# Order of the first four tiles, place of the third tile's v, and of the pad copies, in a fused attention and FFN kernel

## The chip, the cores and the metric

The kernel runs on one core of a Trainium2 chip. The metric is the device time of one execution in microseconds, as the median of several runs; lower is better. Engine names are those of the profile: PE is TensorE (PEld its weight loads), DVE is VectorE, ACT is ScalarE, POOL is GpSimd, SP is SyncE, which here only issues DMAs. A line number such as L169 is a line of the kernel before the change.

## What is computed

A transformer block of one sequence of S = 2048 rows of D = 448 in bfloat16: layer norm without parameters, then attention and a gated FFN in parallel, and the residual. There are 16 heads of 28; a query sees itself and the 255 keys before it. F is 1792.

```python
xn = (x - mean(x)) / sqrt(var(x) + 1e-5)
q, k, v = split(xn @ wqkv)                        # 16 heads of 28
scores = q @ k.T * 28 ** -0.5
scores = where((i - j >= 0) & (i - j < 256), scores, -1e9)
o = softmax(scores) @ v
out = x + o @ wo + (gelu(xn @ w_gate) * (xn @ w_up)) @ w_down
```

## The kernel before

The sequence is cut into 16 tiles of 128 rows and four blocks of 512 rows (`qb`). For each block the program runs attention (L561) and then the gated part of the FFN (`gated`, L452); the products with `wo` and `w_down` of a block run inside the attention of the next. The order of the instructions is written out by hand: each engine takes its own in the order of the program and stops at the first that has to wait. Each score step of attention makes scores (`sc`) in one PSUM tile of 4 banks, of which there is one during attention, and ScalarE turns them into `p_sb` with one exp of 128x2048. The entries of `plan` (L783) say what else is issued in a step, after its exp and its masks: a pair of a generator and a number takes that many pieces of the generator, a function is called.

*One tile's way.* `stat(t)` (L152) is a `bn_stats` and a `bn_aggr` on VectorE. `rstd(t, n)` (L157) is a Ln and an Exp on ScalarE, which give the inverse deviation of n tiles. `norm(t)` (L164) is a `tensor_scalar` on VectorE; for tiles over 3 there is a second one of 64 columns, on GpSimd for tiles 5, 6 and 7. Tiles 0 to 3 are then transposed by five PE instructions and copied out of PSUM by `transp` (L177), alternately through the banks "b2" and "b3", on ScalarE for tiles 0 to 2 and on VectorE for tile 3. Later tiles are transposed by a DMA on the SP queue, `dma_transp` (L173). `v_dense(t)` (L219) makes a tile's v from the first 384 of 448 input columns with three matmuls into a bank, `v_half` (L222) adds the last 64, and `v_copy` (L225) writes the result to `v_sb` and gives the bank back. `proj`, `qk_halves` and `qk_copies` do the same for q and k of a group of four heads; `pads` (L681) copies a group's weight columns into a layout of 32 columns a head.

*The start of the program (L692 to L740).* Ten matmuls on zeros (`warmup`), then tiles 0 to 3. In the order of the program the deviation of tile 2 comes after the transpose and copy of tile 0, that of tile 3 after the copy of tile 1. The pads of group 0 and the lower part of `w3p` stand between the normalizations and the last copy. GpSimd makes the masks after a small memset on VectorE (L716). `swap(0)` and the load of x tiles 8 to 11 are issued when tile 3 is transposed. The third tile's `v_dense` follows, then q and k of group 0, the statistics of tiles 4 and 5 and their deviations.

*The first block's steps.* Step 0 takes q and k of group 1 from `gen_qk` (L272), with both v halves of tiles 2 and 3 ahead of the q/k halves and the copy of tile 3's v after them; `ahead` normalizes and transposes tile 4. Step 1 takes group 2; `ahead2` has the statistics of tiles 6 and 7, tile 5's normalization and transpose, and the copy of tile 2's v. Step 2 takes group 3 and the first pieces of `gen_up`; its own exp stands behind `rstd(6, 2)` (L638); `ahead3` normalizes and transposes tiles 6 and 7 and then calls `loads` (L759), which issues on the SP queue, in this order: the rest of `w_up`, x tiles 12 to 15, `w_gate` in two parts (two DMAs each, one for each half of the partitions), `wo` and `w_down`. The masks of a step in the first block are `affine_select`s on GpSimd (L558), issued behind the step's exp and ahead of its plan. Step 3 ends `gen_up`; v of tiles 4 and 5, 6 and 7 comes from `gen_v` (L229). When attention of the block is over, `gated` starts with `up(0)` and `gate(0)`, whose matmuls `gt` read `wg`.

*Counters of DMAs.* The program's DMAs share eight completion counters in turn; a queue holds a DMA back until the earlier one of the same counter is complete.

Of the kernel before, what the change touches and what calls it, by code (L numbers as in the profile page):

```python
# [13 lines left out]
f32 = mybir.dt.float32  # L14
i32 = mybir.dt.int32

S, D, H, Dh, F = 2048, 448, 16, 28, 1792
P = 128
NT = S // P
NF = F // P  # L20
QB, NB = 512, 4
# [5 lines left out]
def kernel(  # L27
# [118 lines left out]
    def warmup(n):  # L146
        wps = phase[0].pool.tile([P, 2, QB], f32, name="wps", tag="s")
        for i in range(n):
            nc.tensor.matmul(wps[:, i % 2, :], lhsT=warm[:, 0:P], rhs=warm[:, 0:QB], start=True, stop=True)  # L149
# [7 lines left out]
    def rstd(t, n):  # L157
        lnv = work.tile([P, 4], f32, name="lnv")
        nc.scalar.activation(out=lnv[:, 0:n], in_=mv_all[:, t:t + n, 1], func=ACT.Ln, bias=eps_t[:, 0:1], scale=1.0)
        nc.scalar.activation(out=rstd_all[:, t:t + n], in_=lnv[:, 0:n], func=ACT.Exp, scale=-0.5)  # L160
# [61 lines left out]
    def v_half(t, pv):  # L222
        mm_half(pv, xnT[:, 3, t * P:(t + 1) * P], wv[:, 3, :], t % 2, False, True)

    def v_copy(t, pv, copy):  # L225
        copy(out=v_sb[:, t, :, 0:Dh], in_=pv.rearrange("p (h d) -> p h d", d=Dh))
        give(pv)
# [44 lines left out]
    def gen_qk(gs, others):  # L272

        for g in gs:
            pq = take("pq")
            proj(pq, wqp, 0, g)
            yield 650
            pk = take("pk")
            proj(pk, wkp, 0, g)
            yield 650  # L280
            for t, pv in others:
                v_half(t, pv)
            qk_halves(0, g, pq, pk)
            if others:
                v_copy(*others[1], nc.vector.tensor_copy)
            qk_copies(0, g, pq, pk)
            others = ()
            yield 360

    def fill_pads(last):  # L290
# [270 lines left out]
    def attention(qb, plan):  # L561
# [54 lines left out]
        for i, (scores, ncol, edges) in enumerate(steps):  # L616
            assert (qb, scores[-1][0]) in done
            if i in pvs:
                pv(pvs[i])
            while fresh:  # L620
                apply_masks(*fresh.pop(0))
            if not qb and i - 1 in pvs:
                sums()
                inverse()
            if qb == 3 and i - 1 in pvs:
                sums()
            ss = phase[0].pool.tile([P, 4, QB], f32, name="sc", tag="s")
            p_sb = work.tile([P, 4, QB], bf16, name="p_sb", bufs=5)
            for g, half, kt, q0, nq, col in scores:
                k0, nk = (64 * half, 64) if half is not None else (0, P)  # L630
                for j in range(4):
                    r = slice(32 * j, 32 * j + Dh)
                    nc.tensor.matmul(ss[k0:k0 + nk, j, col:col + nq], lhsT=kT[r, g, kt * P + k0:kt * P + k0 + nk],  # L633
                                     rhs=qT[r, g, ring(qb).start + q0:ring(qb).start + q0 + nq], start=True, stop=True,
                                     tile_position=(32 * j, k0), skip_group_check=True)
                parts.setdefault(g, []).append((half, kt, q0, nq, col, p_sb))
            if not qb and i == 2:
                rstd(6, 2)  # L638
            nc.scalar.activation(out=p_sb[:, :, 0:ncol], in_=ss[:, :, 0:ncol], func=ACT.Exp, scale=SCALE)  # L639
            flush()  # L640
            if qb:
                fresh.append((p_sb, edges))
            else:
                for m in edges:
                    masked(p_sb, *m)
            while later:
                scale_o(*later.pop(0))
            for n in plan[i]:
                if n == "sums":
                    sums()  # L650
                elif n == "inverse":
                    inverse()
                if not isinstance(n, tuple):
                    if callable(n):
                        n()
                    continue
                for _ in range(n[1]):
                    next(n[0], None)
            if qb == 3 and i - 2 in pvs:
                inverse()  # L660
# [28 lines left out]
        for _ in gen:  # L689
            pass  # L690

    warmup(10)  # L692
    stat(0)
    rstd(0, 1)
    stat(1)
    rstd(1, 1)
    norm(0)
    transp(0, nc.scalar.copy, "b2")
    stat(2)
    norm(1)  # L700
    rstd(2, 1)
    warmup(1)
    transp(1, nc.scalar.copy, "b3")
    stat(3)
    rstd(3, 1)
    pvs = [take("pv", D)]
    v_dense(0, pvs[0])
    norm(2)
    pads(nc.vector.tensor_copy, wqp, slice(0, 1))
    transp(2, nc.scalar.copy, "b2")  # L710
    pvs.append(take("pv", D))
    v_dense(1, pvs[1])
    norm(3)
    pads(nc.scalar.copy, wkp, slice(0, 1))
    nc.vector.tensor_copy(out=w3p[:, :, 0:Dh], in_=wraw[:, 3, 0:D].rearrange("p (h d) -> p h d", d=Dh))
    nc.vector.memset(masks[:, 0, 0, 0:1], 1.0)  # L716
    make_masks()
    transp(3, nc.vector.tensor_copy, "b3")
    swap(0)
    nc.sync.dma_start(out=x_sb[:, 8:12, :], in_=xv[:, 8:12, :])  # L720
    pvs.append(take("pv", D, "b2"))
    v_dense(2, pvs[2])
    pq, pk = (phase[0].pool.tile([P, 2, QB], f32, name="s0", tag="s")[:, 0, :] for _ in range(2))
    proj(pq, wqp, 0, 0)
    proj(pk, wkp, 0, 0)
    stat(4)
    stat(5)
    rstd(4, 2)
    qk_halves(0, 0, pq, pk)
    for t in range(2):  # L730
        v_half(t, pvs[t])
# [12 lines left out]
        dma_transp(4)  # L744

    def ahead2():
        stat(6)
        stat(7)
        norm(5)
        dma_transp(5)  # L750
        v_copy(2, pvs[2], nc.vector.tensor_copy)

    def ahead3():
        for t in (6, 7):
            norm(t)
            dma_transp(t)
        loads()
# [15 lines left out]
    for qb in range(NB):  # L773
        if qb in (1, 3):
            tc.mark_branch_hint_location("general", hint="LikelyTaken",
                                         engines=[mybir.EngineType.DVE if qb == 1 else mybir.EngineType.PE])
        early = ()
        if qb == 0:
            new_hT(0)
            early = (1, 2, 3)  # L780
            u = chain(gen_qk((1, 2, 3), [(t, pvs[t]) for t in (2, 3)]), gen_up(0, (1, 2)), gen_v(4, False), gen_up(0, (3,)),
                      gen_v(6, True), gen_qk_next())
            plan = [[(u, 2), ahead, (u, 1)], [(u, 2), ahead2, (u, 1)], [lambda: spare.append(spare.pop(1)), (u, 2), ahead3, (u, 4)],  # L783
                    [(u, 11), lambda: fill_pads(False)], [lambda: stat(8), (u, 10), lambda: fill_pads(True)], [(u, 3)],
                    [lambda: stat(9), (u, 4)], [lambda: stat(10), (u, 3)], [lambda: stat(11), (u, 3), lambda: rstd(8, 4)]]
        else:
            d = gen_down(qb - 1)
            if qb < 3:
                u = gen_pairs(qb + 1)
                plan = [[(d, 14)], [(d, 11)], [(d, 11)], [(u, 7)], [(d, 18)], ["sums", (u, 7), "inverse"], [(u, 12)],  # L790
                        [(u, 9)], [lambda: q_last(qb + 1, nc.vector.tensor_copy), (d, 5), "sums", "inverse"], [(d, 13)]]
                if qb == 1:
                    plan[0].append(lambda: rstd(12, 4))
            else:
                new_hT(3)
                early = (1, 2, 3, 4, 5, 6)
                u = gen_up(3, early)
                plan = [[(d, 14)], [(d, 4), (u, 5)], [(u, 9)], [(u, 7)], [(d, 18)], [(u, 7)], [(d, 13)], [(d, 5), (u, 7)],
                        [(u, 7)], [(d, 18)]]
        if qb in (1, 2):  # L800
            swap(qb + 1)
        if qb == 1:
            swap_weights(wvs, wv, wv)
            swap_weights(wsq, wqp, wkp)
            swap(1)
        score_pool(1)
        rest, after, flush = attention(qb, plan)
        nc.scalar.preload_act_table(ACT.Gelu_apprx_tanh)
        score_pool(2)
        if qb not in hTs:  # L810
            new_hT(qb)

        def hook(f):
            after(f)
            if qb < 3 and f == 4:
                collect(qb + 1)
            if qb < 3 and f == 10:
                deliver(qb + 1)
            t = 4 * qb + 8 + f // 2 - 2 * qb
            if qb < 2 and 4 * qb + 8 <= t < 4 * qb + 12:  # L820
                norm(t)
                dma_transp(t)
                if qb == 0:
                    stat(t + 4)

        gated(qb, early, rest, flush, hook)
        if qb < NB - 1:
            nc.scalar.preload_act_table_set("natural_log_exp_and_others")
# [151 lines left out]
```

## Time and profile before

| | us |
|---|---|
| median of 3 runs | 217.25 |
| lowest, highest of them | 216.87, 217.26 |
| the profiled execution | 217.55 |
| span of its instructions | 215.8 |
| PE busy (share of the span) | 210.3 (97%) |
| DVE busy | 156.8 (73%) |
| ACT busy | 131.6 (61%) |
| POOL busy | 48.1 (22%) |
| granted TensorE clock, mean | 0.999 |

The span runs from the first to the last instruction of one profiled execution; times in the lists below count from its start. A row of the timeline holds start, duration, engine, line, operation, what is written and read, and a count where like rows are merged; in brackets stand the idle time of the engine before it and what ended it. SPq is the queue that issues DMAs: its row is the issue, not the transfer. A row of the table by stretches holds, for PE, PEld, DVE, ACT and POOL, the busy time with the number of instructions, then the granted clock, the share of time in which the 16 DMA engines were busy, and GB/s.

### The profile page before, as it was taken

Reading aid. Unit: us, or ns where it says so; the run is one execution under the profiler, and the core shown is the slowest. Engines: PE = TensorE matmul, PEld = TensorE weight load, DVE = VectorE, ACT = ScalarE, POOL = GpSimd, SP = SyncE. Lnnn points to the kernel's source line nnn. Section 1 sums busy time; section 2 is a strip of 40 time slices with the busy share of each in tenths; the row PEclk is TensorE's granted clock in tenths of the full one; section 3 lists DMA queues with packets and bytes.
Section 4 is the critical chain, followed back from the end, with each engine's and each line's share of the span. In section 5 each row is a group of like instructions: output and inputs, shape, how many; then the busy total and the mean of one; then the engine's idle time right before and its main releaser. Section 6 shows DMA issues by size and latency. Waiting matters only on the chain.

```text
span 215.8 us, 6282 instructions
## 1 busy us (share of the span) xinstructions
PE 210.3 (97%) x2688; PEld 102.4 (47%) x2693; DVE 156.8 (73%) x348; ACT 131.6 (61%) x125; POOL 48.1 (22%) x81
## 2 busy tenths in 40 slices
PE   7999999999999999999999999999999999999993
PEld 2433433444445445444445545544444444444892
DVE  7788879799446997598547799567359699587621
ACT  4589589645876976613777797423578676466000
POOL 5278978520000202022000112022000021115001
PEclk9999999999999999999999999999999999999999
DMA  6993499993392000003330000200000000000011
GB/s 185 268 233 47 86 223 230 230 251 70 59 251 70 24 3 28 17 3 50 70 97 24 24 0 3 61 6 3 0 13 11 26 3 24 21 3 0 21 35 42
DMA packets 23553, 15.21 MB, mean 70 GB/s; under 512 B 9856, under 2 KB 23264, under 8 KB 23520
## 3 DMA queue, kind: packets, MB, share of 16 engines
q1 hardware_dynamic: 22576, 14.47, 29.1%
q8 instruction: 22, 0.36, 0.7%
q10 hardware_dynamic: 944, 0.29, 0.5%
q14 instruction: 11, 0.09, 0.1%
HBM read 8.69 MB, written 2.18 MB: 50 GB/s over the span
## 4 chain that ended last, share of the span: by engine, by line
PE 96%; ACT 2%; issue 1%; DVE 0%; DVEq 0%; ACTq 0%
PE po L392 26%; PE gt L432 20%; PE u L432 14%; PE ue L432 7%; PE sc L633 6%; PE ov L600 5%; PE pq L366 4%; PE pv L352 3%; PE pv L190 2%; PE wps L149 2%; PE pq L190 2%; ACT p_sb L639 2%; PE pk L190 1%; PE s L190 1%; PE pq L196 1%
## 5 line engine op out<-in xcount | busy, mean ns | idle before, releaser
L639 ACT ACTIVATE p_sb<-sc 128x2048 bf16<-128x2048 f32 x39 | 73.3, 1878 | 20.3 <-PE sc L633 14.8
L567 POOL TENSOR_TENSOR oN<-oc,l 128x512 bf16<-128x512 f32 x16 | 22.2, 1386 | 140.3 <-DVE l L580 140.3
L471 ACT ACTIVATE ge<-gt 128x1024 bf16<-128x1024 f32 x28 | 28.6, 1023 | 39.1 <-PE gt L432 33.9
L392 PE MATMUL po<-wd,hT 128*128 128x448 bf16 (+1 forms) x266 | 47.9, 324 | 0.0
L432 PE MATMUL gt<-xnT,wg 64*128 64x512 bf16 x224 | 45.4, 376 | 0.0
L432 PE MATMUL gt<-xsw,wg 64*128 64x512 bf16 x168 | 40.6, 376 | 0.0
L479 DVE TENSOR_TENSOR hT<-ge,u 128x512 bf16<-128x512 bf16 x38 | 24.5, 680 | 17.9 <-PE u L432 10.1
L548 DVE TENSOR_TENSOR p_sb<-p_sb,masks 128x256 bf16<-128x256 bf16 (+1 forms) x90 | 30.2, 389 | 5.9 <-ACT p_sb L639 5.9
L392 PEld LDWEIGHTS <-hT 128*128 128x128 bf16 x266 | 24.6, 98 | 16.0 <-issue 1.0
L432 PE MATMUL u<-xnT,wu 64*128 64x512 bf16 x152 | 31.7, 376 | 0.0
L432 PEld LDWEIGHTS <-wg 64*128 64x128 bf16 x392 | 19.6, 94 | 21.9 <-issue 0.2
L432 PEld LDWEIGHTS <-wu 64*128 64x128 bf16 x392 | 19.1, 94 | 23.0 <-issue 3.3
L432 PE MATMUL u<-xsw,wu 64*128 64x512 bf16 x114 | 27.2, 376 | 0.0
L400 DVE TENSOR_TENSOR res<-po,x_sb 128x448 bf16<-128x448 f32 (+1 forms) x17 | 10.1, 593 | 18.8 <-PE po L392 18.8
L633 PE MATMUL sc<-qT,kT 28*64 28x320 bf16 (+7 forms) x648 | 16.4, 261 | 0.3 <-ACT p_sb L639 0.2
L558 POOL TENSOR_SCALAR_AFFINE_SELECT p_sb<-p_sb 128x512 bf16<-128x512 bf16 (+1 forms) x21 | 14.2, 702 | 4.5 <-ACT p_sb L639 4.4
L432 PE MATMUL ue<-xnT,wu 64*128 64x512 bf16 x72 | 15.1, 377 | 0.0
L392 PE MATMUL po<-wo,oN 128*128 128x448 bf16 (+1 forms) x76 | 15.1, 323 | 0.0
L633 PEld LDWEIGHTS <-kT 28*64 28x64 bf16 (+1 forms) x648 | 7.7, 102 | 12.4 <-issue 10.8
L432 PE MATMUL ue<-xsw,wu 64*128 64x512 bf16 x54 | 13.5, 378 | 0.0
L448 DVE CAST hT<-ue 128x512 bf16<-128x512 f32 x18 | 11.5, 682 | 2.4 <-PE ue L432 2.4
L573 DVE STREAM_TRANSPOSE l<-oc 128x512 f32<-128x512 f32 x16 | 11.3, 705 | 1.6 <-POOL oN L567 1.6
(103 smaller groups left out, 253.3 us busy)
## 6 DMA issues: line engine op xcount, KB each, us to landing
out_dram<-res SPq DMA_DIRECT2D x15, 112.0 KB
xsw<-xnT SPq DMA_DIRECT2D x8, 192.0 KB
x_sb<-in_A_x_dram SPq DMA_DIRECT2D x3, 448.0 KB
wu<-in_B_w_up_dram SPq DMA_DIRECT2D x4, 336.0 KB
wd<-in_B_w_down_dram SPq DMA_DIRECT2D x3, 448.0 KB
wg<-in_B_w_gate_dram SPq DMA_DIRECT2D x2, 448.0 KB
wg<-in_B_w_gate_dram SPq DMA_DIRECT2D x2, 336.0 KB
wraw<-in_A_wqkv_dram SPq DMA_DIRECT2D x2, 252.0 KB
```

Of the source, the lines that this page charges most:

```text
L190: nc.tensor.matmul(ps, lhsT=lhs(c), rhs=rhs(c), start=start and c == 0, stop=stop and c == 2, skip_group_check=True)
L392: nc.tensor.matmul(po[:, a:b], lhsT=x[:, k, cs], rhs=wt[:, k, lo + a:lo + b], start=(n == a == 0), stop=(n == len(terms) - 1), skip_group_ ...
L432: nc.tensor.matmul(ps, lhsT=w[64 * hi:64 * hi + 64, c, p * P:(p + 1) * P], rhs=xchunk(qb, hi, c, qb * QB, QB), start=c == 0, stop=c == 6, ...
L448: nc.vector.tensor_copy(out=hTs[qb][:, p + 7 * i, :], in_=us[i])
L471: nc.scalar.activation(out=ges[p][:, :, :], in_=gt[:, :, :], func=ACT.Gelu_apprx_tanh)
L479: nc.vector.tensor_tensor(out=hT[:, p + 7 * i, :], in0=ge[:, i, :], in1=u, op=ALU.mult)
L548: nc.vector.tensor_tensor(out=reg, in0=reg, in1=m, op=ALU.mult)
L558: nc.gpsimd.affine_select(out=reg, in_=reg, pattern=mid + [[1 if diag else -1, min(w, P)]], compare_op=ALU.is_ge, fill=0.0, base=0 if diag ...
L567: nc.gpsimd.tensor_tensor(out=oN[:, g, :], in0=oc[:, :], in1=inv, op=ALU.mult)
L573: nc.vector.transpose(out=l1[:, :, :].rearrange("p a b -> p (a b)"), in_=oc[:, :])
L633: nc.tensor.matmul(ss[k0:k0 + nk, j, col:col + nq], lhsT=kT[r, g, kt * P + k0:kt * P + k0 + nk], rhs=qT[r, g, ring(qb).start + q0:ring(qb) ...
L639: nc.scalar.activation(out=p_sb[:, :, 0:ncol], in_=ss[:, :, 0:ncol], func=ACT.Exp, scale=SCALE)
```

## The change

Seven edits, all in the first some 20 us of the program:

- the warm-up has nine matmuls, not ten;
- statistics and deviation of tile 2 come ahead of the transpose and copy of tile 0, those of tile 3 ahead of the copy of tile 1;
- normalization of tile 3 and the transposes of tiles 2 and 3 come ahead of the second tile's v; the pads, the copy into `w3p` and the masks move behind the normalizations, the last two behind q and k of group 0;
- the third tile's `v_dense` leaves the start and is issued in score step 1; its v half and its copy go with the q/k halves of group 2 (the list of pairs in `gen_qk` becomes a table by group);
- tile 5's statistics leave the start for `ahead2`, its normalization and its transpose leave `ahead2` for `ahead3`;
- the deviations are taken for tile 4 alone at the start and for tiles 5 to 7 together at step 2;
- `swap(0)` and the load of x tiles 8 to 11 stand earlier in the program.

```diff
-            for t, pv in others:
-                v_half(t, pv)
+            if g in others:
+                v_half(*others[g])
             qk_halves(0, g, pq, pk)
-            if others:
-                v_copy(*others[1], nc.vector.tensor_copy)
+            if g in others:
+                v_copy(*others[g], nc.vector.tensor_copy)
             qk_copies(0, g, pq, pk)
-            others = ()
...
             if not qb and i == 2:
-                rstd(6, 2)
+                rstd(5, 3)
...
-    warmup(10)
+    warmup(9)
     stat(0)
     rstd(0, 1)
     stat(1)
     rstd(1, 1)
     norm(0)
+    stat(2)
+    rstd(2, 1)
     transp(0, nc.scalar.copy, "b2")
-    stat(2)
     norm(1)
-    rstd(2, 1)
+    stat(3)
+    rstd(3, 1)
     warmup(1)
     transp(1, nc.scalar.copy, "b3")
-    stat(3)
-    rstd(3, 1)
     pvs = [take("pv", D)]
     v_dense(0, pvs[0])
     norm(2)
+    transp(2, nc.scalar.copy, "b2")
+    norm(3)
     pads(nc.vector.tensor_copy, wqp, slice(0, 1))
-    transp(2, nc.scalar.copy, "b2")
+    transp(3, nc.vector.tensor_copy, "b3")
+    pads(nc.scalar.copy, wkp, slice(0, 1))
+    swap(0)
+    nc.sync.dma_start(out=x_sb[:, 8:12, :], in_=xv[:, 8:12, :])
     pvs.append(take("pv", D))
     v_dense(1, pvs[1])
-    norm(3)
-    pads(nc.scalar.copy, wkp, slice(0, 1))
+    pvs.append(take("pv", D, "b2"))
+    pq, pk = (phase[0].pool.tile([P, 2, QB], f32, name="s0", tag="s")[:, 0, :] for _ in range(2))
+    proj(pq, wqp, 0, 0)
+    proj(pk, wkp, 0, 0)
     nc.vector.tensor_copy(out=w3p[:, :, 0:Dh], in_=wraw[:, 3, 0:D].rearrange("p (h d) -> p h d", d=Dh))
     nc.vector.memset(masks[:, 0, 0, 0:1], 1.0)
     make_masks()
-    transp(3, nc.vector.tensor_copy, "b3")
-    swap(0)
-    nc.sync.dma_start(out=x_sb[:, 8:12, :], in_=xv[:, 8:12, :])
-    pvs.append(take("pv", D, "b2"))
-    v_dense(2, pvs[2])
-    pq, pk = (phase[0].pool.tile([P, 2, QB], f32, name="s0", tag="s")[:, 0, :] for _ in range(2))
-    proj(pq, wqp, 0, 0)
-    proj(pk, wkp, 0, 0)
     stat(4)
-    stat(5)
-    rstd(4, 2)
+    rstd(4, 1)
...
     def ahead2():
-        stat(6)
-        stat(7)
-        norm(5)
-        dma_transp(5)
-        v_copy(2, pvs[2], nc.vector.tensor_copy)
+        for t in (5, 6, 7):
+            stat(t)
 
     def ahead3():
-        for t in (6, 7):
+        for t in (5, 6, 7):
             norm(t)
             dma_transp(t)
         loads()
...
-            u = chain(gen_qk((1, 2, 3), [(t, pvs[t]) for t in (2, 3)]), gen_up(0, (1, 2)), gen_v(4, False), gen_up(0, (3,)),
+            u = chain(gen_qk((1, 2, 3), {1: (3, pvs[3]), 2: (2, pvs[2])}), gen_up(0, (1, 2)), gen_v(4, False), gen_up(0, (3,)),
                       gen_v(6, True), gen_qk_next())
-            plan = [[(u, 2), ahead, (u, 1)], [(u, 2), ahead2, (u, 1)], [lambda: spare.append(spare.pop(1)), (u, 2), ahead3, (u, 4)],
+            plan = [[(u, 2), ahead, (u, 1)], [lambda: v_dense(2, pvs[2]), (u, 2), ahead2, (u, 1)], [lambda: spare.append(spare.pop(1)), (u, 2), ahead3, (u, 4)],
```

## The prediction, made before the changed kernel was run

> **What bounds the kernel now.** The profiled execution took 217.55 us, its span is 215.8 us, so 1.75 us lie around the span; the median of the three timed runs is 217.25 us. I make the sum against the profile and carry its difference over to the median. I read the page's busy times (PE 97% of the span) and its chain first, then the timelines of TensorE, ScalarE, GpSimd and the SP queue through the first 40 us, where the change is.
>
> ```profile
> PE 96%; ACT 2%; issue 1%; DVE 0%; DVEq 0%; ACTq 0%
> ```
>
> TensorE is the bound: the chain of waits is PE but for 2% of ScalarE, and these are the first two exps (13.15 to 17.45 us). After 17.45 us PE has no idle time that the page counts beyond 53 ns, up to its last matmul at 212 us. So a microsecond won or lost at, say, 38 us arrives at the end whole, and one won before 17 us arrives only if nothing later waits on something else. Here is the second score step and the start of the third (PE), then ScalarE beside it:
>
> ```profile
> 15.08 0.40 PE L633 MATMUL sc<-qT,kT 28*128 28x384 bf16 x8
> ...
> 16.86 0.39 PE L196 MATMUL pq<-xnT,w3p 64*128 64x512 bf16 x1
> ...
> 17.45 0.40 PE L633 MATMUL sc<-qT,kT 28*128 28x128 bf16 x8 [0.20 <-ACT p_sb L639]
> ```
> ```profile
> 15.52 1.88 ACT L639 ACTIVATE p_sb<-sc 128x2048 bf16<-128x2048 f32 x1
> 17.30 0.58 ACT L256 CAST qT<-pq 128x512 bf16<-128x512 f32 x1
> 17.76 0.31 ACT L159 ACTIVATE lnv<-mv_all,eps_t 128x2 f32<-128x2 f32 x1
> ...
> 18.21 1.86 ACT L639 ACTIVATE p_sb<-sc 128x2048 bf16<-128x2048 f32 x1
> ```
>
> Scores are written to one buffer, so sc of step 2 waits for the exp of step 1 to end (17.40). PE had finished step 1 at about 17.08, so it stood some 0.37 us: that is all the room the second step has. The third exp starts only at 18.21, behind the qT copy and the deviation of tiles 6 and 7.
>
> Next the chain that the reader would not look at, because none of it is on the critical chain: GpSimd, then SP.
>
> ```profile
> 19.31 0.77 POOL L169 TENSOR_SCALAR xn<-x_sb,mv_all,rstd_all 128x64 bf16<-128x64 bf16 x1
> 20.14 1.23 POOL L558 TENSOR_SCALAR_AFFINE_SELECT p_sb<-p_sb 128x512 bf16<-128x512 bf16 x2
> ```
> ```profile
> 20.11 1.20 SPq L175 DMA_TRANSPOSE xnT<-xn  x1
> 21.97 1.19 SPq L175 DMA_TRANSPOSE xnT<-xn  x1
> 23.26 1.21 SPq L175 DMA_TRANSPOSE xnT<-xn  x1
> 24.52 0.63 SPq L81 DMA_DIRECT2D wu<-in_B_w_up_dram  x1
> ...
> 28.55 0.62 SPq L81 DMA_DIRECT2D wg<-in_B_w_gate_dram  x1
> ...
> 38.00 0.39 SPq L771 DMA_DIRECT2D wd<-in_B_w_down_dram  x1
> ```
> ```profile
> 38.04 0.59 PE L432 MATMUL u<-xnT,wu 64*128 64x512 bf16 x3
> 38.47 0.38 PE L432 MATMUL gt<-xnT,wg 64*128 64x512 bf16 x1
> ```
> ```profile
> 26.00:27.00 1.00, 1.00 (x14) 0.34 (x14) 0.23 (x1) 0.33 (x1) 1.00 (x2) 1.00 0.55 124
> 28.00:30.00 2.00, 2.00 (x31) 0.72 (x30) 1.93 (x5) 2.00 (x3) 0.52 (x1) 1.00 1.05 270
> ```
>
> Tile 5's normalization ends on GpSimd at 20.08 and its transpose is issued at 20.11; tile 6's waits for GpSimd's share of its normalization (21.97; two such from 21.36, 1.14 us together), tile 7's follows on the queue (23.26), and behind it on the same queue stand the weight loads of the FFN (24.52 on). In the table by stretches the last two columns are the share of the DMA engines' time and GB/s: 0.55 in 26 to 27 us, full from 28 on. From there the loads run at the engines' rate. The second half of the first gate weights (issued 28.55) is marked complete in the trace at 37.98; the row of wd at 38.00, which reuses its counter, shows the same. Gate matmuls need both halves and start at 38.47, right behind u. **The slack is 0.49 us.**
>
> **The change, part by part.**
>
> *One warm-up matmul less.* They are 0.427 us apart, so the tenth frees 0.43 us. The ninth has streamed by 5.19; tile 0's xn is ready at 5.15 and its weights load until 5.34, so its transposes run 5.34 to 6.11 in place of 5.62 to 6.39. A shorter warm-up could leave the array at half rate for longer: in the trace 512 columns take 0.427 us up to 6.3, and 448 columns 0.19 us from 7.40. There is no idle stretch of PE in between, before or after the change, so I take nothing; the other bound is rival 3. The Trainium skill ("TensorE: Matmul & The Clock Gate", Part 1) has it that full rate comes after about 3.4 us of sustained activity, in windows that run free of the kernel. This trace took 6.0 us from its first matmul, so the page's figure is not met here. By its rule one matmul less without a gap costs nothing, and a missed window would keep 3.4 us more of work at half rate.
>
> *Deviations first (tiles 2, 3).* Ln and Exp take 0.53 us (4.91 to 5.44). Tile 2's statistics end at 5.91, so ScalarE is in its Exp until 6.48 and copy 0 starts at about 6.4, as before (6.43): the warm-up's gain is spent there. Tile 3's go 6.98 to 7.5, copy 1 at about 7.45 (7.51). On VectorE the two waits for a deviation (0.53 and 0.50 us) go: xn of tile 2 at 6.9 and of tile 3 at 7.55, a microsecond earlier than 8.56. PE: first v 7.15, tp2 7.75, tp3 8.2 (its PSUM bank waits for copy 1), second v 8.65, q/k from 9.25, their half contractions 10.6 where they stood at 11.44. That is 0.85 us: 0.6 is the third v taken out (9.46 to 10.05), 0.25 the rest. The pads behind normalization (0.27 us each) now fill VectorE's wait for tp3; if they did not fit they would cost those 0.27. Masks start on GpSimd at 9.35 (9.22) and end at 14.25 by their 4.88 us, just as the first exp ends. xsw and x 8 to 12 are issued at 10.3 as before, since SP is busy until 10.27. The wk columns of group 1 complete at 12.21 and would be copied at 12.4: no wait, by 0.2 us. So the first exp starts at **12.3 in place of 13.15**.
>
> *Third v in the second step.* Step 1 begins at 14.2. On PE it is now 0.38 (scores) + 0.57 (v) + 1.39 (q, k up to the halves) + 0.2 (v half) + 0.22 (halves) = 2.8 us, so sc of step 2 goes at 17.0 (17.45 before), not at exp 1's end (16.55): PE is the bound of this step, and 0.40 of the 0.85 is given back. qT copy 17.2 to 17.8, deviation of tiles 5 to 7 after it, third exp at **18.1, against 18.21**: another 0.35 given back, as before the copies overlapped PE's wait. Three statistics in this step take 3 x 0.75 on VectorE, from 15.1 to 17.4, so they are in time; with less lead than 0.3 us they would hold up the exp, since Ln stands ahead of it. From there PE is ahead by 0.1 us.
>
> *Tile 5 moved to the third step.* Its statistics, normalization and transpose leave ahead2 for ahead3; the count of instructions is the same. But on GpSimd its 64 columns now stand behind the selects of step 2, which wait for the third exp (ends 19.97): selects 20.04 to 21.27, then 0.57 us to 21.84. Its transpose is issued at 21.87 (+1.76), the others 1.29 us apart on the queue at 23.16 and 24.45, and the loads at 25.71: **+1.19 us**. Tile 5 is complete 2.42 us after its issue (20.11 to 22.53 by the marks), so at 24.29; PE wants it at 24.4. Tile 7: 26.87, wanted at 27.8. These still fit, the first by 0.1.
>
> *Where the stall goes.* The DMA engines are not full before 28 us, so a later start moves the whole row of loads: gate weights complete at 37.98 + 1.19 = 39.17. PE comes at 38.37 and waits 0.8 us; the gate starts 0.70 us later than before, 0.75 with the wake-up of a wait (0.05 in the rows). Nothing behind it has a fixed date that gives it back: the remaining gate weights complete at 42.2 and would at 43.4, wanted at 44.5.
>
> **Sum:** -0.85 (front) + 0.40 (v in step 1) + 0.35 (the exp's place behind qT and deviation) = -0.1 at the third exp; +0.85 at the gate; **+0.75 in all**. Profile 217.55 + 0.75 = 218.3 us; median 217.25 + 0.75 = **218.0 us**. Bounds of what the trace does not show: the third exp may start 0.15 us later than I put it (tp3 waiting longer), GpSimd's 64 columns may take the 0.77 of the first row, not 0.57 (three times, of which one counts): +1.1 at most. If the engines catch up half of the 1.19 by working off the backlog: +0.15. The likeliest case's own range is 217.4 to 218.4.
>
> **Rivals.** (1) *Loads in time.* If the gate weights come at 38.4 or before, because the backlog runs faster without gaps, only PE's 0.1 us is left: 217.15. For it: the share in 26 to 27 is 0.55; against: it is the start that moves, and from 28 on the share is full. (2) *The front carries through.* If the v in step 1 fits into PE's waits and exps start 0.7 us sooner from end to end, loads would be late by 0.5 us only, which the slack takes: 217.25 - 0.7 = 216.55. Against it: PE's room in step 1 is 0.37 us, the v takes 0.57 plus 0.2. (3) *The clock opens later.* If the array stays at half rate through v and q/k of the front (7.15 to 10.6 in the plan above), these 3.45 us of work take twice that, exps and loads come as much later, and the gate at +0.75 + 3.4: 221.4. PE's unbroken row of matmuls from 1.37 us speaks against it. (This is the missed window of the skill's page.) (4) *Other way than said:* the copies are not earlier at all, as computed; this is in the sum.
>
> **Chances.** Forecast 0.70, rival 1 0.18, rival 2 0.09, rival 3 0.03. A measurement of this kernel tells no change from 0.2%, 0.43 us. Forecast and rival 3 give slower, less 0.03 where the forecast comes out under 217.68: 0.70; same 0.18 + 0.03 = 0.21; faster 0.09. The range 217.0 to 218.7 takes in rival 1 and the bounds, and leaves out rivals 2 and 3.
>
> **What would show it.** First exp at 12.3, third at 18.1; the transpose of tile 5 at 21.9 and the first load behind it at 25.7; idle time of PE ahead of the first gt, with a start at 39.2. Loads issued by 25.0, or gt following u without a gap, would make the forecast wrong.

## The result and the profile after

| | before | changed |
|---|---|---|
| median of 7 runs, us | 217.26 | 218.67 |
| lowest, highest | 216.74, 217.86 | 217.92, 219.0 |
| profiled execution, us | 217.55 | 219.0 |
| its span, us | 215.8 | 217.3 |

The ratio of the runs is 1.006, with a 95% interval of 1.0039 to 1.0082: the change makes the kernel slower by 0.85 to 1.8 us. 218.0 us was predicted, from 217.0 to 218.7: the measured median is 0.03 us inside that range, and above the 217.4 to 218.4 that the prediction gave for its likeliest case. The profiled execution of the changed kernel is the slowest of its seven, so the waits below are at the long end.

The chain of waits of the changed kernel (shares of the span by engine) is no longer PE alone:

```profile
PE 83%; DMA 6%; DVE 4%; SPq 2%; POOL 2%; issue 1%; ACT 0%; DVEq 0%; POOLq 0%
```

Read along in time, these are pieces of the same chain up to the first gate (start, length, what):

```profile
19.27 0.61 DVE kT L257
...
20.48 0.63 POOL p_sb L557
21.11 1.14 POOL xn L169 x2
...
24.45 1.09 SPq L175
...
25.59 0.63 SPq L81
...
29.61 10.48 DMA wg<-in_B_w_gate_dram
40.09 0.05 issue
40.14 1.68 PE gt L431 x13
```

The chain runs where the prediction laid it: selects, then normalization on GpSimd, the transposes and the loads on the SP queue, and at the end one long DMA, the second half of the first gate weights, which releases PE at 40.09. As what released the selects the profile names the kT copy on VectorE, which ends at 19.88. The third exp ends at 19.82, and in each of the twelve profiles of this case these selects start 0.06 to 0.08 us behind the end of that exp, in the kernel before while the kT copy is still running (19.92 to 20.60, selects at 20.14): it is the exp that they wait for, as predicted. The timeline of PE at that place:

```profile
37.76 0.59 PE L431 MATMUL u<-xnT,wu 64*128 64x512 bf16 x3
38.58 0.39 PE L431 MATMUL gt<-xnT,wg 64*128 64x512 bf16 x1 [0.23 <-DMA wg<-in_B_w_gate_dram]
40.14 0.39 PE L431 MATMUL gt<-xsw,wg 64*128 64x512 bf16 x2 [1.17 <-DMA wg<-in_B_w_gate_dram]
```

u ends at 38.2 where it ended at 38.5 before. The first gt waits for the first half of the weights, the next for the second half. The pair started together at 38.47 before; now its second matmul comes 1.67 us later. From there to its last matmul PE takes 173.76 us in both profiles, so all 1.67 reach PE's end. The span grows by 1.45 only, since the stretch behind PE's last matmul is 0.22 shorter.

GpSimd, ScalarE and the SP queue in the changed kernel, to be held against the rows before:

```profile
19.89 1.23 POOL L557 TENSOR_SCALAR_AFFINE_SELECT p_sb<-p_sb 128x512 bf16<-128x512 bf16 x2 [1.55 <-DVE kT L257]
21.11 1.70 POOL L169 TENSOR_SCALAR xn<-x_sb,mv_all,rstd_all 128x64 bf16<-128x64 bf16 x3
```
```profile
12.19 1.88 ACT L638 ACTIVATE p_sb<-sc 128x2048 bf16<-128x2048 f32 x1 [0.27 <-PE sc L632]
...
17.03 0.58 ACT L256 CAST qT<-pq 128x512 bf16<-128x512 f32 x1 [0.59 <-PE pq L196]
17.52 0.30 ACT L159 ACTIVATE lnv<-mv_all,eps_t 128x3 f32<-128x3 f32 x1
...
17.96 1.86 ACT L638 ACTIVATE p_sb<-sc 128x2048 bf16<-128x2048 f32 x1
```
```profile
21.72 1.20 SPq L175 DMA_TRANSPOSE xnT<-xn  x1
...
25.59 0.63 SPq L81 DMA_DIRECT2D wu<-in_B_w_up_dram  x1
...
40.11 0.39 SPq L765 DMA_DIRECT2D wd<-in_B_w_down_dram  x1
```

The first exp is at 12.19. Three pieces of 64 columns stand in a row behind the selects, tile 5's transpose goes out at 21.72 (20.11 before), the loads start at 25.59 (24.52). The third exp is at 17.96. The GpSimd engine is idle for 1.55 us ahead of the selects: it was free for tile 5 and had it behind the wrong instruction.

### The profile page after: what moved, and what is told of

The parts are those of the page before. It is cut to its first block, busy times and chain, and to the rows that moved or that the text cites. A ratio compares the mean times of both kernels' runs of the same rounds, so it can differ in the third digit from the quotient of the medians.

```text
span 217.3 us, 6287 instructions
## 1 busy us (share of the span) xinstructions
PE 210.0 (97%) x2692; PEld 101.6 (47%) x2692; DVE 156.1 (72%) x348; ACT 131.8 (61%) x125; POOL 48.0 (22%) x81
## 4 chain that ended last, share of the span: by engine, by line
PE 83%; DMA 6%; DVE 4%; SPq 2%; POOL 2%; issue 1%; ACT 0%; DVEq 0%; POOLq 0%
PE po L391 26%; PE gt L431 20%; PE u L431 13%; PE sc L632 5%; DMA wg<-in_B_w_gate_dram 5%; PE ue L431 4%; PE pq L365 4%; PE ov L599 4%; PE pv L351 3%; DVE st L154 2%; SPq L81 1%; DMA x_sb<-in_A_x_dram 1%; POOL p_sb L557 1%; PE pq L190 1%; PE pv L190 1%
## 5 line engine op out<-in xcount | busy, mean ns | idle before, releaser
L547 DVE TENSOR_TENSOR p_sb<-p_sb,masks 128x256 bf16<-128x256 bf16 (+1 forms) x90 | 30.1, 389 | 5.9 <-ACT p_sb L638 5.9
```

The costliest lines, as they stand in the source:

```text
L547: nc.vector.tensor_tensor(out=reg, in0=reg, in1=m, op=ALU.mult)
```

## Experiments

Ratios are against the kernel before on the same chip; the 95% interval stands in brackets.

**Tile 5 put back into the changed kernel.**

```diff
-    rstd(4, 1)
+    stat(5)
+    rstd(4, 2)
...
-                rstd(5, 3)
+                rstd(6, 2)
...
     def ahead2():
-        for t in (5, 6, 7):
-            stat(t)
+        stat(6)
+        stat(7)
+        norm(5)
+        dma_transp(5)
...
     def ahead3():
-        for t in (5, 6, 7):
+        for t in (6, 7):
```

> The changed kernel with tile 5 alone put back: its statistics and deviation at the start, its normalization and transpose in step 1. Theory (the stall at the first gate comes from tile 5's later transpose, which puts the loads 1.1 us later): the transposes are issued at about 19.0, 21.7, 23.0, the loads from 24.3 (25.59 in the changed kernel, 24.52 before), the second half of the first gate weights is complete by 38.8, gt starts between 38.2 and 38.8, and the time is 216.9 to 217.5, 0.9985 to 1.001 of the kernel before. Rival (the front's new order itself makes the loads late, by what it does to the DMA engines): gt still starts at about 40 and the time stays at 218.3 to 218.9.

Measured: 217.36 us, ratio 1.0009 (0.9999 to 1.0019). The SP queue and PE:

```profile
19.28 1.20 SPq L175 DMA_TRANSPOSE xnT<-xn  x1
21.84 1.19 SPq L175 DMA_TRANSPOSE xnT<-xn  x1
24.40 0.63 SPq L81 DMA_DIRECT2D wu<-in_B_w_up_dram  x1
```
```profile
37.87 0.59 PE L431 MATMUL u<-xnT,wu 64*128 64x512 bf16 x3
38.30 0.38 PE L431 MATMUL gt<-xnT,wg 64*128 64x512 bf16 x1
```

The transposes have their gap again (19.28, 21.84), the loads start at 24.40 and gt follows u without a wait. The loss is gone (the interval leaves 0.4 us at most), so it came from tile 5. The front's own order brings no gain that this can show.

**Tile 5 moved in the kernel before, and nothing else** (normalization and transpose only).

```diff
     def ahead2():
-        norm(5)
-        dma_transp(5)
...
     def ahead3():
-        for t in (6, 7):
+        for t in (5, 6, 7):
```

> The kernel before, with nothing changed but tile 5's normalization and transpose, which go from step 1 to step 2. Theory: third exp at 18.2 as before, transpose of tile 5 at 22.0, loads from 25.8, the second half of the first gate weights complete at 39.3 to 40.4, gt at the same, time 218.1 to 219.2 (1.004 to 1.009). Rival (the move costs nothing by itself, since the DMA engines have room up to 28 us): loads 1.3 us later, but gt at 38.5 and 217.0 to 217.5.

Measured: 218.79 us, ratio 1.0079 (1.006 to 1.0098). Loads from 25.31, and PE:

```profile
38.09 0.39 PE L432 MATMUL gt<-xnT,wg 64*128 64x512 bf16 x1
39.70 0.39 PE L432 MATMUL gt<-xsw,wg 64*128 64x512 bf16 x2 [1.22 <-DMA wg<-in_B_w_gate_dram]
```

Two instructions and one DMA moved, none of them on the chain of waits before, make the whole loss in the old kernel too. The rival is out. The third exp was at 17.67 in this profile, not 18.2: see the last section.

**The gate weights first.** The changed kernel, then the kernel before, with the loads in another order:

```diff
         load_ffn(wu, B_w_up, slice(0, 1))
-        load_ffn(wu, B_w_up, slice(4, 7))
-        nc.sync.dma_start(out=x_sb[:, 12:16, :], in_=xv[:, 12:16, :])
         load_ffn(wg, B_w_gate, slice(0, 3))
+        nc.sync.dma_start(out=x_sb[:, 12:16, :], in_=xv[:, 12:16, :])
         load_ffn(wg, B_w_gate, slice(3, 7))
+        load_ffn(wu, B_w_up, slice(4, 7))
```

> The changed kernel with the loads in another order: the rest of w_up's first part, the first gate weights, x 12 to 15, the other gate weights, and the last part of w_up at the end. Theory: the first gate weights are complete by 34.6, PE goes from u into gt without a wait at 38.2, and the 0.3 us that PE is ahead there (38.18 against 38.47) arrive at the end: 216.7 to 217.2, 0.9975 to 1.0. Rival (something other than those weights holds the gate, or a later load takes their place): gt after 39, or waits at the fourth gate (43 us) or at the later u (46 us); 217.6 or more.

> The kernel before with the same order of loads as the third kernel. Theory: nothing waited there, so nothing changes: 0.999 to 1.001 of before, 217.1 to 217.5, and the third kernel is faster than it by the front's 0.3 us. Rival (the order of the loads is what wins, the front nothing): this one is as fast as the third kernel.

Measured: the changed kernel 217.2 us, ratio 1.0001 (0.9989 to 1.0012); the kernel before 217.38 us, ratio 1.0003 (0.999 to 1.0016). The weights are complete at 35.95 in the first (34.6 was expected) and gt starts at 38.12: a wait for those weights and nothing else held PE. The 0.35 us that PE is then ahead of 38.47 do not arrive in this profile, which is that of the slowest of its 11 executions (217.89). The row of gt, and a later one of its PE timeline that shows why:

```profile
38.12 0.38 PE L431 MATMUL gt<-xnT,wg 64*128 64x512 bf16 x1
...
62.88 0.36 PE L351 MATMUL pv<-wv,xnT 64*128 64x448 bf16 x1
63.34 0.36 PE L351 MATMUL pv<-wvs,xsw 64*128 64x448 bf16 x2
```

The last of these matmuls waits for `wvs`, complete at 63.30, the next date that the SP queue sets. In the kernel before it is complete at 62.99 and PE comes at 63.25: a second place with little slack. It took something in this profile alone: in the other eleven, PE takes 173.74 to 173.77 us from the gate matmul that needs the second half to its last matmul, here 174.16. The expectation of 0.3 us against the reordered kernel before fell: the intervals lie on each other.

**The 64 columns on VectorE.** In the changed kernel `norm` takes VectorE for all tiles:

```diff
-        both = ((nc.vector, 0, D, 0), (nc.gpsimd if t in (5, 6, 7) else nc.vector, D, 64, 384))
+        both = ((nc.vector, 0, D, 0), (nc.gpsimd if False else nc.vector, D, 64, 384))
```

> The changed kernel with the 64-column part of the normalization of tiles 5 to 7 on VectorE, not on GpSimd. Theory (what delays tile 5 is its place behind the selects of step 2 on GpSimd): the transposes are issued at about 18.9, 20.2 and 21.5, the loads from 22.8, the first gate weights are complete by 37.5, PE goes into gt without a wait: 217.0 to 217.5, 0.998 to 1.001 of before. Rival (the loads end at the same time whenever they start, because the DMA engines are the limit): a wait at gt remains, 218 or more.

Measured: 217.15 us, ratio 0.9998 (0.9985 to 1.001). Tile 5 stays in step 2, but no longer stands behind the selects:

```profile
18.97 3.83 SPq L175 DMA_TRANSPOSE xnT<-xn  x3
22.85 2.66 SPq L81 DMA_DIRECT2D wu<-in_B_w_up_dram  x4
```

So it is not the step that delays tile 5 but the queue of GpSimd in that step. The edit takes tiles 6 and 7 off GpSimd too, so the loads start 1.7 us sooner than in the kernel before; the weights were complete at 36.15, 1.8 us sooner than there, and gt started at 38.26 without a wait.

**Part of the loads in the idle stretch.** The changed kernel with two of the loads issued in step 1:

```diff
     def ahead2():
+        load_ffn(wu, B_w_up, slice(4, 7))
         for t in (5, 6, 7):
...
         load_ffn(wu, B_w_up, slice(0, 1))
-        load_ffn(wu, B_w_up, slice(4, 7))
```

> The changed kernel with the two DMAs of the last part of w_up issued in step 1, ahead of the transposes, when the DMA engines are idle (about 17 to 21 us). Theory: these 672 KB leave the row of loads after 25.6 us, so that the second half of the first gate weights is complete 2 to 3 us sooner, at 37 to 38, gt starts at 38.2 without a wait: 216.9 to 217.4, 0.998 to 1.001. Rival (the early load delays tile 5's transpose and the v of tile 5 waits instead): a wait of PE near 24.2, 217.5 to 218.5.

Measured: 217.1 us, ratio 0.9998 (0.9983 to 1.0013). The queue's later rows are those of the changed kernel; the 672 KB went out at 15.09 and were complete at 20.9:

```profile
15.09 1.30 SPq L81 DMA_DIRECT2D wu<-in_B_w_up_dram  x2
21.71 3.83 SPq L175 DMA_TRANSPOSE xnT<-xn  x3
25.60 1.28 SPq L81 DMA_DIRECT2D wu<-in_B_w_up_dram  x2
```

Gate weights complete at 35.62 and gt at 38.17. With the transposes as late as in the changed kernel the loss is gone: the lateness matters through the amount of load that stands ahead of the gate weights. The weights came sooner than expected (37 to 38), and the time is still that of the kernel before: with the loads out of the way these runs show nothing more to win.

**The third v back at the start**, in the first experiment's kernel:

```diff
     pvs.append(take("pv", D, "b2"))
+    v_dense(2, pvs[2])
...
-[lambda: v_dense(2, pvs[2]), (u, 2), ahead2, (u, 1)]
+[(u, 2), ahead2, (u, 1)]
```

> The first experiment (tile 5 put back) with the third tile's v_dense also back at the start, ahead of q and k; its half and its copy stay in step 1. Theory (moving the v into step 1 only trades 0.6 us at the start for the wait of the step, and the exp of step 2 stands behind the same copy and deviation): first exp 0.6 later than in the first experiment, third exp within 0.3 of it, time within 0.3 of it: 217.1 to 217.6, 0.9995 to 1.002. Rival (the moved v is worth its 0.6 us): 217.9, 1.003 or more.

Measured: 217.2 us, ratio 1.0001 (0.9988 to 1.0014). The first exp is at 12.80 against 12.31 in the first experiment, the third at 18.02 against 18.08. Half a microsecond at the first exp is gone by the third: the place of this v brings nothing that these runs can tell (0.3 us either way).

**Fewer warm-up matmuls in the kernel before**: `warmup(9)`, twice, and `warmup(8)`.

> The kernel before with nine matmuls in the first warm-up. Theory: tile 0 is transposed and copied up to 0.3 us sooner, the third exp and with it PE come at most 0.3 us sooner, and it arrives at the end: 216.9 to 217.3, 0.9985 to 1.0. Rival (one matmul less leaves the array at half rate a window longer): 219 or more. A third way: nothing moves, since tiles 2 and 3 wait for their deviations anyway, 217.2 to 217.4.

> The kernel before with eight matmuls in the first warm-up. Theory: the ninth already ended within 0.05 us of tile 0's xn, so an eighth end leaves PE idle for 0.4 us and gains nothing on nine: 216.7 to 217.0, as the kernel before with nine. Rival (with a gap in the row the array opens to full rate later in some executions): the times spread more, 217.0 to 218 or a median over that of nine.

> The kernel before with nine matmuls in the first warm-up, once more beside eight. Theory: 216.7 to 217.1, 0.997 to 0.9995 of before. Rival (the first measurement of it was chance): 217.2 to 217.4, 0.9995 to 1.001.

Measured: nine 216.85 us, ratio 0.9984 (0.997 to 0.9998), and again 216.93 us, 0.9993 (0.9984 to 1.0001); eight 216.9 us, 1.0001 (0.9985 to 1.0016). The two measurements of nine lie in one direction and the second reaches 1: by the ratios a gain of 0.15 to 0.35 us, not beyond doubt. Eight has the same median; its ratio of 1.0001 carries one execution of 218.53. ScalarE in the first of these shows an order that the changed kernel gives up:

```profile
5.77 0.58 ACT L186 COPY xnT<-tp 128x512 bf16<-128x512 bf16 x1 [0.34 <-PE tp L185]
```

Here tile 0's copy starts as soon as its transposes end. In the changed kernel it comes behind tile 2's deviation:

```profile
5.96 0.29 ACT L159 ACTIVATE lnv<-mv_all,eps_t 128x1 f32<-128x1 f32 x1 [0.50 <-DVE mv_all L155]
6.29 0.20 ACT L160 ACTIVATE rstd_all<-lnv 128x1 f32<-128x1 f32 x1
6.40 0.57 ACT L186 COPY xnT<-tp 128x512 bf16<-128x512 bf16 x1
```

The date 5.77 is not the missing matmul's doing alone: with ten warm-up matmuls, in the profile of tile 5 moved alone, this copy starts at 5.76, where the array came to its full rate early (last section). Eight and nine warm-up matmuls in the kernel before have the lowest medians found.

## Why the prediction was right, and where a size was off

*The mechanism held; that the time lies in the range is in part luck.* Tile 5 behind the selects of step 2 on GpSimd, transposes in one row on SP, the loads behind them, PE waiting at the first gate: the profile has each of them, moving tile 5 alone in the old kernel makes the loss, and putting it back, taking GpSimd out of its way, reordering the loads or thinning them out each takes the loss away.

*Step by step.* The first exp was put at 12.3 and came at 12.19; sc of step 2 at 17.0 and 16.93; the third exp at 18.1 and 17.96. Tile 5's transpose was put at 21.87 and issued at 21.72, the loads at 25.71 and 25.59 (+1.07 for +1.19). That "a later start moves the whole row of loads" held for 15 of the 16 parts into which each load is split: by the completion marks the 15th part of the second half came at 36.90 before and at 37.90 now.

*The term that was mis-sized* is the last part of that load. It was taken to keep its distance, so "gate weights complete at 37.98 + 1.19 = 39.17". It came at 40.09, 2.19 us behind the 15th where it was 1.08 behind before. So the weights came 2.11 us later, 1.00 by the later start and 1.11 by the last part; less the slack of 0.49 and with 0.05 for the wake-up, the gate is 1.67 us later in the profile, in place of 0.75. The later start, the one term that the prediction had, makes 0.56 of it. The time is 1.3 us more (ratio) in place of 0.75. For the last part the prediction had no term, and its bound of "+1.1 at most" was passed; that the median still lies in the range, by 0.03 us, is luck. The place of the wait was foreseen, its form not: in place of one start at 39.2, the first gt came at 38.58 and the second at 40.14, each behind its own half of the weights.

In the twelve profiles the last part is 0.04 to 1.3 us behind the 15th where the loads start by 24.5 us or are thinned out (before, tile 5 back, reordered before, on VectorE, early part, third v back, the warm-ups) and 1.55 to 2.19 where they start after 25 in full (changed, tile 5 alone, gate weights first). Each trace has a 16 KB transfer of instructions among the loads, which takes 0.9 to 1.3 us; it falls at 30.1 to 30.7 us in the three with the long distance, but at 30.2 in the early-part kernel too, where the distance is 0.17. In the changed kernel the distance grows from 0.18 to 1.55 us between the marks at 29.40 and 33.12, across that transfer, and to 2.50 at 37.15, where no such transfer stands. Why one part falls so far behind in the late group was not tried and stays open. That late loads cost more than the later start is not an accident of one execution: both kernels that have them in the old order, the changed one and tile 5 moved alone, are 1.3 and 1.7 us slower over all their runs.

*The front.* The prediction let -0.1 us of it reach the third exp. Between the two profiles it is -0.25 there and -0.29 at the end of u. But the timed kernels with the changed front and no late loads (1.0009, 1.0001, 0.9998, 0.9998, 1.0001) show none of it, with intervals of 0.2 to 0.3 us either way. What they agree with is the give-back in the second step: 0.85 us at the first exp (0.96 in the profiles) are a quarter of that two exps later, and the third v's place alone shows no gain. A part of what the profiles show is the clock (last section).

*The warm-up.* The prediction saw "no idle stretch of PE" after the change. In the changed kernel's profile PE stands idle for 0.42, 0.20 and 0.24 us ahead of the transposes of tiles 0 and 1 and the first v: the array was at full rate from about 4.1 us, so its warm-up ended early. Nothing was lost by it, since ScalarE came to copy 0 at 6.40, as predicted.

*The rivals.* Loads in time (217.15) is what the kernels without the late loads measure. The front did not carry through. A clock that opens a window later because of the missing matmul shows in no profile: full rate came at 4.0 to 7.2 us with eight or nine warm-up matmuls and at 4.6 to 7.3 with ten.

## What to carry to other kernels

An engine with little to do has a queue all the same: before an instruction is moved past others on it, follow what waits for it through the other queues, to the date at which the bound engine wants the last thing in the row. Here GpSimd was idle for 1.55 us just ahead, and two moved instructions and a DMA cost more than 1 us through 15 us of DMA row. A DMA counts as complete with its slowest part (here 40.09, with 15 of 16 parts done at 37.90): slack against a load in a full row is read from the last mark, and can shrink by more than the start moves. Time won at the front is worth what the next wait leaves of it; ask for the second date (here `wvs` at 63 us) too.

## What the runs showed of the hardware

The array's full rate came at a different time in each profile: the distance of the warm-up's matmuls of 512 columns falls from 0.427 to 0.216 us, or a transpose's length from 0.314 to 0.219, at between about 4.0 us (gate weights first) and about 7.3 us (kernel before), 2.7 to 5.9 us after the first matmul, with nothing in the programs to explain it. The granted clock in the profile's table by stretches reads 1.00 through this time, so the slow start shows in the rows alone. The kernel before and those with its front and ten warm-ups reached gt (or the end of u) at 38.47, 38.34 and 38.09 us with the rate open at 7.3, 6.0 and 4.6 us; those with the changed front at 38.1 to 38.3 whether it opened at 4.0 or 7.2. A single pair of profiles compares such fronts with an error of 0.4 us; the prediction worked from a profile with a late opening. The Trainium skill ("TensorE: Matmul & The Clock Gate", Part 1) says that the windows run free of the kernel, with which these profiles agree; its spread of 0.5 us either way is less than theirs, while the 6, 11 or 14 slow matmuls that it counts for one kernel are nearer to them (six of the warm-up in the changed kernel, all ten in the kernel before).
